# Spectral block and squared-ReLU layer: the middle part with pair 0's casts on ScalarE, pair 6's stage 4 from Z, pair 7's stage 4 by sums, and written orders

## The chip, the cores and the metric

One core of a Trainium2 chip. The metric is the device time of one execution in microseconds (us), the median of several runs. A profile covers one execution; its span runs from the first to the last instruction. Below, PE is TensorE, DVE is VectorE, ACT is ScalarE, POOL is GpSimd, and SP issues the DMAs.

## What is computed

The input is x, 2048 rows of 512 (bf16). The first half is a layer norm, a two-dimensional real Fourier transform over rows and columns, a product with a complex weight for each frequency, the transform back, and x added. The second half is a layer norm and a dense layer with a squared ReLU, and its input added.

```
def _A_ref(x, w_r, w_i):
    X = jnp.fft.rfft2(x.astype(jnp.float32), axes=(-2, -1))
    X = X * (w_r + 1j * w_i)
    return jnp.fft.irfft2(X, s=(S, D), axes=(-2, -1)).astype(jnp.bfloat16)
def _B_ref(x, w1, b1, w2, b2):
    h = jnp.einsum("bsd,df->bsf", x, w1) + b1
    r = jnp.where(h > 0, h, 0)
    return jnp.einsum("bsf,fd->bsd", r * r, w2) + b2
h  = x + _A_ref(_layernorm(x), A_w_r, A_w_i)
h2 = h + _B_ref(_layernorm(h), B_w1, B_b1, B_w2, B_b2)
```

F, the width of the dense layer, is 1792.

## The kernel before, in words

The transforms are products with tables of sines and cosines, which the kernel makes at its start. Rows are held as 128 partitions of 16 groups. The Fourier part has six stages:

- Stage 1 (line 409) multiplies x with a table that also holds the norm's scale, and leaves Bt. Up to about 21 us.
- Stage 2 (line 502, tile p2) and its cast to U (line 514, ScalarE; halves of pairs 0 and 1 on both engines).
- Stage 3 (line 553; pair 0: line 535, tile p3) and its cast to AB or X (lines 543 and 582).
- X by a sum and a difference of AB's halves (line 587, VectorE; pairs 5 to 7 get X from TensorE and skip it), the product m of X with the weights W (line 601, VectorE), Z, the two parts of the complex product (line 613, VectorE), and the folds M, sum and difference of Z's halves (line 621, VectorE; pair 0 has none).
- Stage 4 (line 634, tile p4): products of M with the tables EI; pair 0 reads Z. Its cast to T2 (line 659) is on ScalarE, for pair 7 on ScalarE and VectorE, a small part first (T2a), the rest later.
- Stages 5 and 6 (lines 709 to 807) end the transform and add x; the first two groups have a form of their own. Then the dense layer: line 904 the first product, line 917 the ReLU, line 922 the square, line 933 the second product, line 943 the sum, one DMA out for each group.

The loop of line 488 goes over eight pairs, pair 0 being rows 0 and 8 of the frequency axis and pair p the rows p and 16-p. Stages 2 and 3 of pair 0 and stage 2 of pair 1 are emitted earlier ("first").

The order on each engine is the work of a planner, the class Plan (line 34). Every operation is a task with an engine, an assumed duration, what it reads and writes, a priority and, where it takes a buffer, a pool with a number of buffers ("mm" and "sg" are PSUM, 3 and 2 in the middle; U, X, m, Z and M have 2 buffers each, AB 3). `run` (line 89) takes again and again the task that by its own reckoning can start first; "lag" is what it adds for a DMA's landing. The order in which tasks are taken is the order of the instructions on their engine, and the waits follow from the tiles. Where the planner sees TensorE idle, `warm` (line 235) and `bank` (line 687) put small products of zeros in front of a new PSUM tile, called fillers below, whose number follows from the planned gap. The middle part is everything between the `run` of line 491 and that of line 676. There the planner's order has M of pair 6 on VectorE ahead of pair 7's m, and pair 7's stage 4 (two tiles, one for each value of r) in this form:

```
for lt in (2 * half, 2 * half + 1):
    r, e = lt // 2, lt % 2
    ...
    for u in range(2):
        mm(o, lhsT=mv[:, u, r, e, :], rhs=EI[:, 1 - u:3 - u, pr, :], start=(u == 0), stop=(u == 1))
```

Each tile needs both folds (u is the fold).

Of the kernel before, what the change touches and what calls it, by code (L numbers as in the profile page):

```python
# [9 lines left out]
ALU = mybir.AluOpType  # L10
# [5 lines left out]
P = 128  # L16
# [17 lines left out]
class Plan:  # L34
# [13 lines left out]
    def add(self, eng, w, fn, reads=(), writes=(), prio=0.0, alloc=None, at=0.0, shared=False, lag=0.0,  # L48
            uses=(), order=()):
        many = isinstance(eng, tuple)  # L50
        ways = dict(zip(eng, w)) if many else {eng: w}
        t = dict(many=many, eng=None, ways=ways, w=0.0, fn=fn, reads=list(reads), writes=list(writes), prio=prio, alloc=alloc, at=at,
                 shared=shared, lag=lag, end=None, order=list(order), n=len(self.tasks))
        self.tasks.append(t)
        for k in t["writes"]:
            self.made.setdefault(k, []).append(t)
        for k in set(t["reads"]) | set(t["writes"]) | set(uses):
            self.use.setdefault(k, []).append(t)
# [30 lines left out]
    def run(self):  # L89
        left = {}  # L90
        for t in self.tasks:
            if t["end"] is None:
                for e in t["ways"]:
                    left.setdefault(e, []).append(t)
        for ts in left.values():
            ts.sort(key=lambda t: (t["prio"], t["n"]))
        while any(left.values()):
            best = None
            for e, ts in left.items():
                cand = []  # L100
                for t in ts:
                    r = self.ready(t, e)
                    if r is None:
                        continue
                    if t["alloc"]:
                        s, _ = self.slot(t["alloc"][0])
                        if s is None:
                            continue
                        r = max(r, s)
                    r = max(r, self.free[e])  # L110
                    cand.append((r, t))
                    if r <= self.free[e] + 1e-9:
                        break
                pick = None
                if cand:
                    first = min(r for r, _ in cand) + self.SLACK
                    pick = next(c for c in cand if c[0] <= first)
                if pick and (best is None or pick[0] < best[0] or (pick[0] == best[0] and e == "DVE")):
                    best = (*pick, e)
            if best is None:  # L120
                raise RuntimeError("no task can start: " + str([(list(t["ways"]), t["writes"]) for ts in left.values()
                                                                for t in ts][:6]))
            r, t, e = best
            t["eng"], t["w"] = e, t["ways"][e]
            if t["alloc"]:
                tag, key = t["alloc"]
                _, old = self.slot(tag)
                if old is not None:
                    self.held[tag].remove(old)
                self.held[tag].append(key)  # L130
            self.gap = r - self.free[e]
            t["end"] = r + t["w"]
            self.free[e] = t["end"]
            for k in t["ways"]:
                left[k].remove(t)
            self.log.append((r, t["end"], e, t["writes"]))
            t["fn"](*([e] if t["many"] else []))
# [3 lines left out]
def kernel(  # L141
# [21 lines left out]
    WSC = 2.0 / (S * D)  # L163
    L = D // 2
# [35 lines left out]
    EI = fwd.tile([P, 3, 9, P], BF16, name="EI")  # L200
    CN = fwd.tile([P, 7, P], BF16, name="CN")
# [74 lines left out]
    for i in range(2):  # L276
        add("SP", 1.0, lambda i=i: (sy.dma_start(W[:, i], wv[i][:, 0:8, 1:L + 1]),
                                        sy.dma_start(W[:, 2 + i, 0], wv[i][:, 8, 1:L + 1])), writes=[("Wn", i)],
            prio=8 + i, at=1.0, lag=6.0)
    for i in range(2):  # L280
        add("SP", 1.0, lambda i=i: sy.dma_start(W[:, 2 + i, 1:8], wx[i][:, ::-1]), reads=[("wx", i)], writes=[("Wr", i)],
            prio=10 + i, lag=6.0)
# [163 lines left out]
    def tr_dma(i, dst, src, dep, prio):  # L446
        add("SP", 2.5, lambda: sy.dma_start(dst, src, transpose=True), reads=dep, writes=[("EI", i)], prio=prio, lag=4.0)
# [9 lines left out]
    PE0, PE1, PES = 5, 8, 1  # L457
    BY_PE = tuple(range(PE0, PE1, PES))
    dve(0.25, lambda: ve.tensor_scalar(CN[:, 0:len(BY_PE)], EF[:, 1, PE0:PE1:PES], -1.0, None, ALU.mult), 75.0, reads=["EF1"],
# [11 lines left out]
    def mid_tasks():  # L471
        def b1t():
# [4 lines left out]
            order=["EF2", ("X", 0, 0)], writes=[("EI", 2)])  # L477
        act(1.07, lambda: sin_of(flat(GI[:]), lo(flat(fiI[:]))), 142.0, reads=["fiI"], order=[("p3", 4)], writes=["GI"])
# [9 lines left out]
    for pr, first in ((0, 1), (1, 1), *((p, 0) for p in range(8))):  # L488
# [45 lines left out]
        if pr == 0 and first:  # L534
# [8 lines left out]
            def ea0(u):  # L543
                X = buf(fwd, ("X", 0), "AB", [P, 2, 2, 256], BF16, 3) if u == 0 else T["X", 0]
                COPY[("ACT", "DVE")[u]](flat(X[:, u]), T["p3", 0, u][:])
            for u in range(2):
                add("PE", 0.46, lambda u=u, s3z=s3z: s3z(u), reads=[("U", 0, u), "EF0", "EF1", "EF2"], order=[("p3", 0, j) for j in range(u)],
                    writes=[("p3", 0, u)], prio=z + 1, alloc=("sg", ("p3", 0, u)))
                add(("ACT", "DVE")[u], (0.59, 0.66)[u], lambda u=u, ea0=ea0: ea0(u), prio=z + 1, reads=[("p3", 0, u)],
                    order=[("X", 0, 0)] * u, writes=[("X", 0), ("Xu", u)] + [("X", 0, 0)] * (1 - u),  # L550
                    alloc=None if u else ("AB", ("X", 0)))
        elif pr > 0 and not first:
# [32 lines left out]
            act(0.93, ea, z + 1, reads=[("p3", pr)], writes=[ab], alloc=("AB", ab))  # L585
            if ab[0] == "AB":
# [6 lines left out]
                for h in range(2):  # L593
                    dve(0.34, lambda pr=pr, h=h: bf(pr, h), z, reads=[("AB", pr)],
                        order=[("Xh", pr)] * h,
                        writes=[("X", pr)] + [("Xh", pr)] * (1 - h), alloc=("X", ("X", pr)) if h == 0 else None)
# [9 lines left out]
        for u in range(2) if pr == 0 else ():  # L606
            dve(0.61, lambda u=u, prod=prod: prod(0, u, 1), z, reads=[("Xu", u), ("Wn", 0), ("Wn", 1)], uses=[("X", 0)],
                order=["mh"] * u, writes=[("m", 0)] + ["mh"] * (1 - u), alloc=None if u else ("m", ("m", 0)))
# [7 lines left out]
        for r in range(2):  # L616
            dve(0.34, lambda pr=pr, r=r: zz(pr, r), z, reads=[("m", pr)],
                order=[("Zh", pr)] * r,
                writes=[("Z", pr)] + [("Zh", pr)] * (1 - r), alloc=("Z", ("Z", pr)) if r == 0 else None)
        if pr > 0:  # L620
# [8 lines left out]
            for h in range(2):  # L629
                dve(0.34, lambda pr=pr, h=h: fold(pr, h), z, reads=[("Z", pr)],  # L630
                        order=[("Mh", pr)] * h,
                    writes=[("M", pr)] + [("Mh", pr)] * (1 - h), alloc=("M", ("M", pr)) if h == 0 else None)

        def s4(pr=pr, half=0):
            if pr == 7:
                pt = sg_tile(("p4", pr, half))
            else:
                pt = mm_tile(("p4", pr)) if half == 0 else T["p4", pr]
            for lt in (2 * half, 2 * half + 1):
                r, e = lt // 2, lt % 2  # L640
                k = lt % 2 if pr == 7 else lt
                o = pt[:, 256 * k:256 * k + 256]
                if pr == 0:
                    zv = T["Z", 0][:].rearrange("p u r (j e) -> p u r e j", e=2)
                    for u, k1 in ((0, 0), (1, 8)):
                        ou = o[:, P * u:P * u + P]
                        mm(ou, lhsT=zv[:, u, r, e, :], rhs=EI[:, 1, k1, :], start=True, stop=False)
                        mm(ou, lhsT=zv[:, u, 1 - r, e, :], rhs=EI[:, 2 if r == 0 else 0, k1, :], start=False, stop=True)
                else:
                    mv = T["M", pr][:].rearrange("p u r (j e) -> p u r e j", e=2)  # L650
                    for u in range(2):
                        mm(o, lhsT=mv[:, u, r, e, :], rhs=EI[:, 1 - u:3 - u, pr, :], start=(u == 0), stop=(u == 1))  # L652
        for h in range(2):
            add("PE", 0.46, lambda pr=pr, h=h, s4=s4: s4(pr, h),
                reads=[("M" if pr else "Z", pr), ("EI", 0), ("EI", 1), ("EI", 2)], order=[("p4", pr, 0)] * h,
                writes=[("p4", pr), ("p4", pr, h)], prio=z + 32 * (pr < 5),
                alloc=("sg", ("p4", pr, h)) if pr == 7 else ("mm", ("p4", pr)) if h == 0 else None)

        def et(eng=sc.copy, pr=pr, a=0, b=G, l0=0, l1=4):
            dst = T2[:, l0:l1, a:b, 2 * pr:2 * pr + 2, :].rearrange("p l g q s -> p l q g s")  # L660
            src = T["p4", 7, l0 // 2] if pr == 7 else T["p4", pr]
            eng(dst, src[:].rearrange("p (l q g s) -> p l q g s", q=2, g=G, s=8)[:, :, :, a:b])
        if pr < 7:
            act(0.97, et, z + 3, reads=[("p4", pr)], writes=["T2", "T2a"])
        else:
            for h in range(2):
                eng = ("ACT", "DVE")[h]
                add(eng, (0.24, 0.22)[h], lambda et=et, h=h, eng=eng: et(COPY[eng], 7, 0, 2, 2 * h, 2 * h + 2), prio=z,
                    reads=[("p4", 7, h)], writes=["T2a"])
                add(eng, (0.52, 0.6)[h], lambda et=et, h=h, eng=eng: et(COPY[eng], 7, 2, G, 2 * h, 2 * h + 2), prio=z + 90,  # L670
                    reads=[("p4", 7, h)], order=["T2a"], writes=["T2"])
# [4 lines left out]
    plan.run()  # L676
# [52 lines left out]
    for c, (a, b) in enumerate(CHUNKS):  # L729
# [3 lines left out]
        for g in range(a, b):  # L733
            z = late + g
            if c > 0:
# [18 lines left out]
                for i in range(2):  # L754
                    dve(0.36, lambda g=g, i=i: lv1(g, i), z, reads=[("p5", g), ("od", g)],
                        order=[("qh", g)] * i + [("un", 1)] * (c == 1),
                        writes=[("q", g), ("qh", g)] if i == 0 else [("q", g)], alloc=("qb" if g in BY_PE2 else "q", ("q", g)) if i == 0 else None)
# [16 lines left out]
                else:  # L774
# [11 lines left out]
                    for k in range(4):  # L786
                        dve(0.25, lambda g=g, k=k: lv2(g, k), z, reads=[("q", g)], order=[("Rh", g)], writes=[("R", g)])
# [9 lines left out]
        if c == 0:  # L797
            for g in range(2):
# [9 lines left out]
                for k in range(3):  # L808
# [3 lines left out]
                        writes=[("py", g, k)], prio=-5000.0 + g - 50 * (k == 0), alloc=("sg", ("py", g)) if k == 0 else None)  # L812
# [21 lines left out]
                add(("ACT", "DVE")[g], (0.6, 0.7)[g], un0, reads=[("r2", 0, g), ("n2", 0, g)], writes=[("un", g)] + ["una0"] * (1 - g),  # L834
# [16 lines left out]
        else:  # L851
# [8 lines left out]
            for g in range(a, b):  # L860
                def un(e, g=g, a=a, c=c):
# [9 lines left out]
                    writes=[("un", g)] + [("una", a)] * (g == a), prio=z, shared=True, alloc=("u2", ("u", c)) if g == a else None)  # L871
            for g in range(a, b):
# [3 lines left out]
                def turn(c=c, i=g - a):  # L876
# [3 lines left out]
                    writes=[("UT", c)] + [("UTh", c)] * (g == a), prio=z, alloc=("UT", ("UT", c)) if g == a else None)  # L880
            for g in range(a, b):
# [9 lines left out]
                def et2(e, c=c, g=g, i=g - a):  # L891
# [3 lines left out]
                    writes=[("UT", c)] + [("UTh", c)] * (g == a), prio=z, alloc=("UT", ("UT", c)) if g == a else None)  # L895

        for f in range(NF):
# [24 lines left out]
            def sqr(c=c, f=f, n=n):  # L922
# [4 lines left out]
                writes=[("act", c, f), ("act", c)], alloc=("act", ("act", c)) if f == 0 else None)  # L927
# [53 lines left out]
```

## Time and profile before

| | |
|---|---|
| Time, median of 3 runs | 161.3 us (160.69, 161.30, 161.52) |
| Span of the profiled execution | 159.2 us; the page gives no other time for it |
| TensorE busy | 152.4 us, 1026 products recorded |
| VectorE busy | 120.6 us, 325 instructions |
| ScalarE busy | 102.2 us, 187 instructions |
| GpSimd busy | 32.9 us, 83 instructions |
| Granted TensorE clock | 1.000 over the span |
| Middle part | about 21.5 to 46.4 us of the span |

A row of the timeline gives the start in us, the time it takes, the engine, the line, the operation, out<-in with partitions x elements, how many instructions the row joins (x2), and in brackets the idle time of the engine ahead of it with what ended it. A row of the chain of waits gives start, length and what the time was spent on; "issue" is time in which the engine waited for nothing that the profile shows. A matmul's end is modelled.

### The profile page before, as it was taken

The numbers are of one execution on the slowest core, as the hardware profiler recorded it, in microseconds if no ns is written. First come the engines' busy times: TensorE is split into PE (matmuls) and PEld (weight loads), VectorE is DVE, ScalarE is ACT, GpSimd is POOL, SyncE is SP. The second block draws the span as 40 slices with busy tenths as digits, with TensorE's granted clock in tenths as the row PEclk, the third lists the DMA queues.
The fourth block names the chain that finished last, engine by engine and source line by source line (L and its number), as shares of the span: only waits on it lengthen the run. The fifth ranks groups of instructions, "written<-read, shape, count | busy, mean of one in ns | idle before, by whom it ended". The sixth has DMA issues, their size and how long they took to land.

```text
span 159.2 us, 2899 instructions
## 1 busy us (share of the span) xinstructions
PE 152.4 (96%) x1026; PEld 92.2 (58%) x1035; DVE 120.6 (76%) x325; ACT 102.2 (64%) x187; POOL 32.9 (21%) x83
## 2 busy tenths in 40 slices
PE   6999999999988999999999999999999999999992
PEld 4587876777666876565644544444544444565471
DVE  6999999999967996889863898992599962285221
ACT  8989689998976897297900889530488820188100
POOL 8798700000000024022230004440002240000000
PEclk9999999999999999999999999999999999999999
DMA  5958999992000001102332000224100212010011
GB/s 137 326 185 236 210 272 223 399 353 77 0 4 0 0 4 35 35 33 33 37 64 68 33 0 4 57 44 132 33 2 4 55 43 66 33 35 4 0 66 33
DMA packets 21018, 13.43 MB, mean 84 GB/s; under 512 B 9739, under 2 KB 19723, under 8 KB 21003
## 3 DMA queue, kind: packets, MB, share of 16 engines
q1 hardware_dynamic: 21002, 13.25, 30.7%
q8 instruction: 8, 0.13, 0.4%
q14 instruction: 8, 0.06, 0.1%
HBM read 8.92 MB, written 3.01 MB: 75 GB/s over the span
## 4 chain that ended last, share of the span: by engine, by line
PE 70%; DVE 18%; DMA 4%; issue 3%; SPq 1%; ACT 0%; POOL 0%; DVEq 0%
PE po L936 30%; PE sg L907 20%; PE ph L907 10%; DVE m L605 5%; DMA xs<-in_A_x_dram 4%; DVE Z L615 4%; DVE st L387 3%; DVE M L626 2%; DVE M L628 2%; DVE X L591 2%; PE pp L762 1%; PE pp L769 1%; SPq L266 1%; PE s_p L507 1%; PE s_p L652 1%
## 5 line engine op out<-in xcount | busy, mean ns | idle before, releaser
L936 PE MATMUL po<-W,act 128*128 128x512 bf16 (+1 forms) x229 | 48.7, 366 | 0.5
L919 ACT ACTIVATE rl<-sg,b1f 128x384 bf16<-128x384 f32 (+2 forms) x46 | 27.3, 602 | 21.8 <-PE sg L907 20.6
L907 PEld LDWEIGHTS <-W 128*128 128x128 bf16 x288 | 26.8, 98 | 19.6 <-issue 0.2
L907 PE MATMUL sg<-UT,W 128*128 128x384 bf16 (+2 forms) x184 | 37.2, 337 | 0.0
L936 PEld LDWEIGHTS <-act 128*128 128x128 bf16 x238 | 23.2, 98 | 24.1
L925 DVE TENSOR_TENSOR act<-rl 128x384 bf16<-128x384 bf16 (+2 forms) x70 | 25.0, 366 | 6.5 <-ACT rl L919 6.0
L945 DVE TENSOR_TENSOR ot<-po,hb 128x512 bf16<-128x512 f32 (+1 forms) x17 | 11.2, 659 | 21.0 <-PE po L936 20.7
L854 POOL TENSOR_SCALAR rs<-ss 128x1 f32<-128x1 f32 x14 | 5.5, 394 | 91.5 <-ACT junk L674 91.5
L919 ACT ACTIVATE rl<-ph,b1f 128x512 bf16<-128x512 f32 (+2 forms) x23 | 13.9, 602 | 10.0 <-PE ph L907 9.4
L907 PE MATMUL ph<-UT,W 128*128 128x512 bf16 (+3 forms) x96 | 19.9, 330 | 0.1
L790 DVE TENSOR_TENSOR hs<-pp,xs 128x512 bf16<-128x512 f32 x14 | 9.7, 690 | 2.3 <-PE pp L762 1.3
L674 ACT ACTIVATE junk<-hs,nm 128x512 bf16<-128x512 bf16 x14 | 10.0, 713 | 0.1
L486 PE MATMUL m_p<-U,EF 128*128 128x512 bf16 (+1 forms) x46 | 9.5, 337 | 0.0
L387 DVE BATCH_NORM_STATS2 st<-xs 128x6 f32<-128x512 bf16 x14 | 9.0, 673 | 0.6 <-DMA xs<-in_A_x_dram 0.6
L785 DVE TENSOR_TENSOR R<-q 128x127 bf16<-128x127 f32 x40 | 9.4, 283 | 0.0
L794 DVE TENSOR_TENSOR hb<-hs,b2b 128x512 f32<-128x512 bf16 x14 | 9.2, 683 | 0.0
L237 PEld LDWEIGHTS <-fz 128*128 128x128 bf16 x80 | 6.4, 110 | 4.6 <-issue 2.6
L856 POOL TENSOR_TENSOR rs<-rs,mhalf 128x1 f32<-128x1 f32 x14 | 8.3, 594 | 1.2
L584 ACT CAST AB<-m_p 128x1024 bf16<-128x1024 f32 x7 | 7.1, 1019 | 1.2 <-PE m_p L486 1.1
L752 DVE TENSOR_TENSOR q<-pp,od 128x256 f32<-128x256 f32 x20 | 7.6, 414 | 0.0
L507 PEld LDWEIGHTS <-Bt 128*128 128x128 bf16 x64 | 6.2, 98 | 1.5 <-DVE Bt L442 0.2
L652 PEld LDWEIGHTS <-M 128*128 128x128 bf16 x56 | 5.2, 98 | 3.1 <-DVE M L626 1.4
(160 smaller groups left out, 229.5 us busy)
## 6 DMA issues: line engine op xcount, KB each, us to landing
W<-in_B_w_dram SPq DMA_DIRECT2D x2, 1792.0 KB, 10.5
out_dram<-ot SPq DMA_DIRECT2D x15, 128.0 KB, 1.8
xs<-in_A_x_dram SPq DMA_DIRECT2D x4, 256.0 KB, 3.8
xs<-in_A_x_dram SPq DMA_DIRECT2D x2, 512.0 KB, 6.8
W<-wx SPq DMA_DIRECT2D x2, 448.0 KB
W<-in_A_w_r_dram SPq DMA_DIRECT2D x1, 512.0 KB, 8.2
W<-in_A_w_i_dram SPq DMA_DIRECT2D x1, 512.0 KB, 6.2
wx<-in_A_w_r_dram SPq DMA_DIRECT2D x1, 448.0 KB
```

The source lines that it names most:

```text
L387: ve.bn_stats(st[:], xs[:, g, :])
L486: mm(o.rearrange("p (j i e) -> p j i e", e=2, i=RUN), lhsT=w, rhs=U[:, q, s].rearrange("p (j e i) -> p j i e", e=2, i=RUN), **k)
L674: sc.activation(junk[:], src, ACT.Square, bias=nm1[:, g:g + 1], accum_out=ss2[:, g:g + 1])
L785: ve.tensor_tensor(o, x, y, (ALU.add, ALU.subtract, ALU.subtract, ALU.add)[k])
L790: dve(0.66, lambda g=g: ve.tensor_tensor(hs[:, g, :], T["p6", g][:], xs[:, g, :], ALU.add), z, reads=[("p6", g)], writes=[("hs", g)])
L794: add(("DVE", "POOL")[HBP], (0.62, 1.3)[HBP], lambda g=g: (ve, gp)[HBP].tensor_tensor(hb[:, g, :], hs[:, g, :], b2b[:], ALU.add), prio=lat ...
L856: pool(0.57, lambda p0=p0, p1=p1: gp.tensor_tensor(rs2[:, p0:p1], rs2[:, p0:p1], mhalf[:, 0:p1 - p0], ALU.pow), z, reads=[("sd", c, k)], w ...
L907: mm(p[:, P * i0:P * i1], lhsT=W1[:, d, bass.ts(f, P)], rhs=T["UT", c][:, i0:i1, d, :], start=(d == 0), stop=(d == ND - 1))
L919: sc.activation(r[:, 0:P * n], T["ph", c, f][:, 0:P * n], ACT.Relu, bias=b1f[:, f:f + 1], scale=1.0)
L925: ve.tensor_tensor(t[:, f, 0:P * n], r[:, 0:P * n], r[:, 0:P * n], ALU.mult)
L936: mm(p[:, cs], lhsT=T["act", c][:, f, bass.ts(i, P)], rhs=W2[:, f, cs], start=(f == 0), stop=(f == NF - 1))
L945: ve.tensor_tensor(o[:, cs], T["po", g, h][:, cs], hb[:, g, cs], ALU.add)
```

## The change

It touches the planner and the middle part; the stages before and behind keep their code, and only names are added there.

- Tasks get names, and `run` takes a written order for each engine; the middle part runs by such an order for PE, ACT and DVE.
- Pair 0: both halves of the cast after stage 3 are on ScalarE (before: one on ScalarE, one on VectorE).
- Pair 6 has no folds. Its stage 4 reads Z, with 16 products instead of 8, and needs a negated table EN (128x256), which ScalarE makes from EI. The first part needs only the first half of Z.
- Stage 4 of pairs 1 to 5 and 7 sums over the folds: a first part with M's first half into all outputs, a second part with M's second half. For pair 7 each part is in two pieces, one for each tile.
- The planner's assumed DMA lags change.

```
-                COPY[("ACT", "DVE")[u]](flat(X[:, u]), T["p3", 0, u][:])
+                sc.copy(flat(X[:, u]), T["p3", 0, u][:])
...
+        for pr in BY_Z:
+            act(0.37, lambda pr=pr: sc.activation(EN[:, BY_Z.index(pr)], EI[:, 0:2, pr], ACT.Identity, scale=-1.0), 84.0,
+                reads=[("EI", 0), ("EI", 1)], writes=[("EI", 3, pr)])
...
-        if pr > 0:
+        if pr > 0 and pr not in BY_Z:
             def fold(pr=pr, h=0):
...
-        def s4(pr=pr, half=0):
+        def s4(pr, part, lts):
+            key = ("p4", pr, "t", lts[0] // 2) if pr == 7 else ("p4", pr)
+            pt = T[key] if part else (sg_tile if pr == 7 else mm_tile)(key)
+            src = T["M" if pr and pr not in BY_Z else "Z", pr][:].rearrange("p u r (j e) -> p u r e j", e=2)
+            for lt in lts:
...
+                elif pr in BY_Z:
+                    for u in range(2):
+                        i = 1 if r == part else 0 if u != r else 2
+                        mm(o, lhsT=src[:, u, part, e, :], rhs=EI[:, i:i + 2, pr, :] if i < 2 else EN[:, BY_Z.index(pr)],
+                           start=part == 0 and e == 0 and u == 0, stop=part == 1 and e == 1 and u == 1)
                 else:
+                    mm(o, lhsT=src[:, part, r, e, :], rhs=EI[:, 1 - part:3 - part, pr, :],
+                       start=part == 0 and e == 0, stop=part == 1 and e == 1)
...
+    MID = {
+        "PE": "p2-2-0 p2-2-1 p3-1 p2-3-0 p2-3-1 p3-2 p2-5-0 p2-5-1 p3-3 p2-6-0 b1 p2-4-0 p2-4-1 p3-5 "
+             "p2-6-1 p3-4 p4-0-0 p4-0-1 p4-1-0 p4-1-1 p2-7-0 p2-7-1 p4-2-0 p4-2-1 p3-6 p3-7 p4-3-0 "
+             "p4-3-1 p4-5-0 p4-5-1 p4-4-0 p4-4-1 p4-6-0 p4-6-1 p4-7-0a p4-7-0b p4-7-1a p4-7-1b",
+        "ACT": "U-2 AB-1 U-3 AB-2 U-5 AB-3 EI-2 b1f U-4 AB-5 U-6 AB-4 T2-0 T2-1 U-7 GI EI-3-6 AB-6 T2-2 "
+              "AB-7 T2-3 T2-5 sqrt T2-4 T2-6 T2a-0 T2b-0",
+        "DVE": "m-0-0 m-0-1 Z-0-0 Z-0-1 X-1-0 X-1-1 m-1 X-2-0 Z-1-0 Z-1-1 X-2-1 M-1-0 M-1-1 X-3-0 m-2 "
+              "X-3-1 Z-2-0 Z-2-1 m-3 M-2-0 Z-3-0 Z-3-1 M-2-1 M-3-0 X-4-0 m-5 X-4-1 Z-5-0 Z-5-1 m-4 "
+              "M-5-0 M-5-1 M-3-1 Z-4-0 Z-4-1 m-6 M-4-0 Z-6-0 M-4-1 m-7 Z-6-1 Z-7-0 Z-7-1 M-7-0 M-7-1 "
+              "T2a-1 T2b-1",
+    }
+    plan.run(MID)
```

In a name like M-4-1 the first number is the pair and the second the half; EI-3-6 is the negated table of pair 6.

## The prediction

> **What bounds the kernel now.** I read the share of the span by engine and line first, then the chain of waits between 17 and 50 us, then each engine's instructions in order of time over the stretch that the change touches.
>
> ```profile
> PE 70%; DVE 18%; DMA 4%; issue 3%; SPq 1%; ACT 0%; POOL 0%; DVEq 0%
> PE po L936 30%; PE sg L907 20%; PE ph L907 10%; DVE m L605 5%; DMA xs<-in_A_x_dram 4%; DVE Z L615 4%; DVE st L387 3%; DVE M L626 2%; DVE M L628 2%; DVE X L591 2%; PE pp L762 1%; PE pp L769 1%; SPq L266 1%; PE s_p L507 1%; PE s_p L652 1%
> ```
>
> TensorE carries the last two thirds (the dense layer, lines 907 and 936). The middle, which the change rewrites, hangs on VectorE alone: lines 605, 615, 591, 626 and 628. The chain of waits shows it without a break:
>
> ```profile
> 21.53 0.06 DVE AB L545
> ...
> 24.92 1.24 DVE m L605
> 26.16 0.02 issue
> 26.18 0.77 DVE Z L615 x2
> ...
> 45.02 0.35 DVE M L628
> 45.37 0.04 issue
> 45.42 0.94 PE s_p L652 x7
> 46.36 0.28 PE pp L690 x5
> 46.64 0.76 PE pp L712 x6
> ```
>
> So from 21.53 to 45.36 us the end is set by VectorE, then by pair 7's stage 4, five filler products and stage 5. What the middle gains, the dense layer starts earlier: its weights landed at 32.1 and 38.3 us, so no transfer holds it, and I let the gain pass whole.
>
> The single rows that I use, VectorE and then ScalarE:
>
> ```profile
> 21.53 0.69 DVE L545 CAST AB<-s_p 128x512 bf16<-128x512 f32 x1 [0.18 <-PE s_p L486]
> 22.14 1.28 DVE L605 TENSOR_TENSOR m<-AB,W 128x1024 bf16<-128x1024 bf16 x2
> 23.46 0.76 DVE L615 TENSOR_TENSOR Z<-m 128x512 bf16<-128x512 bf16 x2
> 24.14 0.75 DVE L591 TENSOR_TENSOR X<-AB 128x512 bf16<-128x512 bf16 x2
> 24.92 1.23 DVE L605 TENSOR_TENSOR m<-X,W 128x2048 bf16<-128x2048 bf16 x1
> ```
>
> ```profile
> 21.10 0.59 ACT L545 CAST AB<-s_p 128x512 bf16<-128x512 f32 x1 [0.28 <-PE s_p L486]
> 21.58 1.17 ACT L476 ACTIVATE EI<-EI 128x1152 bf16<-128x1152 bf16 x1
> 22.83 1.01 ACT L584 CAST AB<-m_p 128x1024 bf16<-128x1024 f32 x1
> ```
>
> From such rows: a VectorE operation on 512 elements takes 0.415 us, but the next starts 0.335 after it (the two Z: 0.76 in all); a product m takes 1.215, pitch 1.135; half an m, pitch 0.60; a ScalarE cast of 1024 takes 1.015, pitch 0.91. An operation that needs the result of the one just ahead starts 0.035 after its end, not 0.08 before it (Z ends at 24.22, X began at 24.14; but m ends at 26.15 and its Z starts at 26.18). Such a pair loses 0.115; with a separate wait instruction between, as for the folds at 41.81 and 44.60, 0.18. TensorE starts 128x256 products every 0.109 us and 128x512 ones every 0.216.
>
> **The change, step by step.** Up to 21.3 us the instruction order is unchanged, and on SP's and GpSimd's queues throughout, DMAs included; the new lags only steer the planner.
>
> 1. *Pair 0's second cast leaves VectorE.* It frees 0.61 there. But the first half of m waits for the first cast, which ScalarE still ends at 21.69. For that hand-over I take 0.055, the nearest row being ScalarE to TensorE (a cast ends 24.76, its product starts 24.82): m at 21.74 instead of 22.14, minus 0.40. ScalarE does the second cast at 21.58 to 22.17, in time for 22.34. m, m, Z, Z (0.60, 0.72, 0.335, 0.335) leave VectorE free at 23.74.
>
> 2. *A new stall ahead of X of pair 1.* The written order makes TensorE do both halves of pair 2's stage 2 before pair 1's stage 3: eight products from 21.33, the last ending at 22.37, and ScalarE must cast U of pair 2 first (22.47 with its wait instructions). Only then, 0.91 later, comes pair 1's cast AB, 23.39 to 24.40, against 22.83 to 23.85 before. On VectorE everything is queued behind X: it waits from 23.74 to 24.46, and m of pair 1 starts at 25.25 instead of 24.92: plus 0.33. The 0.40 is gone and more. (The second half of W for this m landed at 24.57, so it doesn't hold it.)
>
> 3. *Pair 6's two folds go:* 2 x 0.335, minus 0.67.
>
> 4. *The written order parts dependent neighbours.* After pair 1's m, the page of before pays 0.115 at two Z behind their m (26.18, 35.99), at M (26.98), at m (34.73) and at Z (43.74), and 0.18 at the M of 41.81 and 44.60: 0.93. In the new order another operation stands between nearly all; only pair 7's M directly follows its Z (0.115). Minus 0.81. Here the Trainium skill speaks against the change: "VectorE: DVE Perf Modes", section "The DRAIN you can't avoid", says that the next operation doesn't start until the pipe is empty and that a semaphore costs nothing extra. By that rule this term is nil, and the sum ends near 161.4. The rows above decide otherwise (X starts 0.08 before Z's end), so I take 0.81.
>
> 5. *Pair 6 reads Z, at a price: a new wait.* In the built program, the second half of pair 6's Z waits for the last product of the first part of its stage 4, which reads the first half; the halves interleave in one tile. VectorE runs without stall from 25.25 through 27 small operations and 7 m: 27 x 0.335 + 7 x 1.135 = 17.0, to 42.27. The wait ends later: pair 4's M ends at 41.21; TensorE, in its written order, does four products of pair 4 (to 41.70) and then pair 6's eight, the last starting at 42.47 and ending at 42.74; Z starts at 42.78. Plus 0.51. Pair 7's Z and M, the end of the stage, are queued behind it.
>
>    The other costs of this edit: eight more products on TensorE (0.87), of which the path sees what the wait holds; the negated table on ScalarE, 128x256, between 0.37 (the EO cast of that size) and 0.47; I take 0.47, hidden by the 1.1 us that AB of pair 6 is early for its m, and up to 0.1 more without that cover.
>
> Together at the last M: 0.33 - 0.67 - 0.81 + 0.51 = -0.64, so about 44.7 instead of 45.36. Adding the new order forward, 42.78 + 3 x 0.335 + 0.115 + 0.335 + 0.418, gives 44.65.
>
> 6. *Pair 7's stage 4 by sums.* Four of its eight products need only the first M. They start at 44.4, so after the second M four are left instead of eight: 0.4 less. But ten filler products (five before) now stand between it and stage 5. The last product ends at 45.45, VectorE's small cast at 45.7, stage 5 could go on at 45.76; the fillers occupy TensorE to 45.84, and its second product, the one that needs VectorE, starts at 45.95. Before, 46.68. Of the 0.4 the fillers and the cast's latency leave about 0.1. T2 of pair 6 on ScalarE (44.33 to 45.34) ends just as pair 7's first tile is ready, so it costs nothing, but has no slack. The swapped EO casts (0.37 against 0.42) are within 0.05 either way; I take nothing. The 21 fillers that go from the middle stood in TensorE's idle time: nothing.
>
> Sum: -0.64 - 0.1 = **-0.7 us**, of a profiled span of 159.2, hence 158.5. The page gives no other time for that execution; the three runs, 160.69 to 161.52, lie 1.5 to 2.3 above this span, which I take as unchanged. On the median 161.3 this makes **160.6 us**, 0.43% less.
>
> **Rivals.**
> - *The hold in step 5 is short or absent* (the sum's only stall behind a product that is done within a few tenths). Then Z follows at 42.3, the stage ends 0.5 earlier, and T2 of pair 6 moves along: -1.2, 160.1. For it: at 41.3 to 42.3 VectorE has a whole m to cover TensorE. Against: the wait is in the program, and the twelve products take 1.3 us by their rows.
> - *ScalarE eats the gain.* It has 0.59 + 0.47 more, and by my sums no idle time from 22.47 to 43.6: 19 casts at 0.91, tables and the table load. X of pairs 2 and 3 have 0.1 and 0.3 us of slack, T2 of pair 6 0.7. Two rows of before show casts of 1.06 and 1.07 (30.45 and 31.36). If all took that, 19 x 0.05 = 0.95 collects, and 0.3 to 0.6 of it lands on the path: 161.1.
> - *ScalarE becomes the bound, slower:* the same engine, with the place at the late casts (T2 of pairs 4 and 6). It decides from a mean pitch above 0.99: 19 x 0.08 = 1.5, less 0.7 of slack, cancels the gain. At 1.05, 19 x 0.14 = 2.7, less 0.7, against -0.7: 162.6. Against it: no cast of before is above 1.07 (pitch 0.96).
>
> **How the numbers follow.** A measurement can tell about 0.5% (0.8 us) from no change, so the limits are 160.5 and 162.1. Main sum: 0.55, spread 160.2 to 161.0, a little under half below 160.5. Short hold: 0.20, all below. ScalarE eats the gain: 0.14, no change. Slower: 0.11. Faster 0.25 + 0.20 = 0.45; same 0.30 + 0.14 = 0.44; slower 0.11. The range 159.8 to 161.5 takes in the first three and the bounds of the hand-over and the table, and leaves most of the last out.
>
> **What would show it.** VectorE idle for 0.7 us before X at 24.5, and 0.5 before a Z near 42.8, ended by TensorE; the last M ending at 44.7; no loss between Z and M elsewhere; the second product of stage 5 near 45.95; ScalarE without idle time from 22.5. I am wrong if pair 1's AB ends before 24.0 (faster), if the dependent pairs cost 0.115 wherever they stand (no gain), or if VectorE waits for ScalarE after 30 us (slower).

## The result, and the profile after

| | before | changed |
|---|---|---|
| Time, median of 4 runs | 161.09 us (160.69 to 161.52) | 160.26 us (159.92 to 160.37) |
| Ratio, 95% interval | | 0.9938 (0.9917 to 0.9960) |
| Span of the profiled execution | 159.2 us | 158.4 us (this execution took 160.21) |
| VectorE / ScalarE busy | 120.6 / 102.2 us | 119.0 / 102.5 us |

The change gains 0.83 us, 0.4 to 0.8% by the interval; 0.7 us was forecast. The shares by engine and line in the changed kernel:

```profile
PE 74%; DVE 15%; DMA 4%; issue 3%; SPq 1%; ACT 1%; POOL 0%; ACTq 0%
PE po L965 31%; PE sg L936 20%; PE ph L936 10%; DMA xs<-in_A_x_dram 4%; DVE Z L624 3%; DVE m L614 3%; DVE st L393 3%; DVE X L600 2%; PE m_p L516 2%; PE pp L788 1%; DVE M L635 1%; PE pp L795 1%; SPq L272 1%; DVE M L637 1%; PE s_p L516 1%
```

VectorE's share of the chain fell from 18% to 15%. TensorE's stage 2 (line 516, "PE m_p") now has 2%; before, one stretch of 0.87 us of it stood in the chain, too little for this list. The chain of waits between 17 and 50 us shows where (start, length, what):

```profile
22.42 0.86 PE m_p L495 x4
23.28 0.89 PE m_p L516 x8
24.17 0.03 ACTq L526
24.20 0.24 ACT AB L593
24.44 0.02 issue
24.46 0.77 DVE X L600 x2
...
41.27 0.61 PE m_p L662 x4
41.88 0.89 PE m_p L659 x8
42.77 0.02 issue
42.79 1.10 DVE Z L624 x3
...
44.40 1.05 PE s_p L662 x8
45.45 0.56 PE pp L716 x10
46.00 0.65 PE pp L738 x6
```

Before, VectorE alone stood in the chain from 21.53 to 45.36. Now the chain leaves it twice, at the two places that steps 2 and 5 named: ahead of X of pair 1 (TensorE and ScalarE, to 24.46) and ahead of the second half of pair 6's Z (TensorE, to 42.79). VectorE's own rows, with the idle time in brackets:

```profile
21.77 1.29 DVE L614 TENSOR_TENSOR m<-AB,W 128x1024 bf16<-128x1024 bf16 x2 [0.36 <-ACT AB L554]
23.09 0.76 DVE L624 TENSOR_TENSOR Z<-m 128x512 bf16<-128x512 bf16 x2
24.46 0.76 DVE L600 TENSOR_TENSOR X<-AB 128x512 bf16<-128x512 bf16 x2 [0.61 <-ACT AB L593]
25.25 1.22 DVE L614 TENSOR_TENSOR m<-X,W 128x2048 bf16<-128x2048 bf16 x1
...
41.13 1.21 DVE L614 TENSOR_TENSOR m<-AB,W 128x2048 bf16<-128x2048 bf16 x1
42.79 1.09 DVE L624 TENSOR_TENSOR Z<-m 128x512 bf16<-128x512 bf16 x3 [0.45 <-PE m_p L659]
43.92 0.42 DVE L635 TENSOR_TENSOR M<-Z 128x512 bf16<-128x512 bf16 x1
44.26 0.42 DVE L637 TENSOR_TENSOR M<-Z 128x512 bf16<-128x512 bf16 x1
```

Between 25.25 and 42.34 no row has a bracket, so VectorE never stands idle there. And ScalarE, where the rivals had placed trouble:

```profile
25.22 1.04 ACT L593 CAST AB<-m_p 128x1024 bf16<-128x1024 f32 x1
26.12 1.06 ACT L526 CAST U<-m_p 128x1024 bf16<-128x1024 f32 x1
27.02 1.07 ACT L593 CAST AB<-m_p 128x1024 bf16<-128x1024 f32 x1
27.93 1.22 ACT L482 ACTIVATE EI<-EI 128x1152 bf16<-128x1152 bf16 x1
```

The casts take 1.04, 1.06, 1.07, yet start 0.90 to 0.91 apart. A row's length is not what the engine pays for it.

### The profile page after: what moved, and what is told of

It is laid out like the page before. It is cut to its first block, busy times and chain, and to the rows that moved or that the text cites. A ratio compares the mean times of both kernels' runs of the same rounds, so it can differ in the third digit from the quotient of the medians.

```text
span 158.4 us, 2890 instructions
## 1 busy us (share of the span) xinstructions
PE 152.0 (96%) x1027; PEld 91.9 (58%) x1027; DVE 119.0 (75%) x322; ACT 102.5 (65%) x189; POOL 33.1 (21%) x83
## 4 chain that ended last, share of the span: by engine, by line
PE 74%; DVE 15%; DMA 4%; issue 3%; SPq 1%; ACT 1%; POOL 0%; ACTq 0%
PE po L965 31%; PE sg L936 20%; PE ph L936 10%; DMA xs<-in_A_x_dram 4%; DVE Z L624 3%; DVE m L614 3%; DVE st L393 3%; DVE X L600 2%; PE m_p L516 2%; PE pp L788 1%; DVE M L635 1%; PE pp L795 1%; SPq L272 1%; DVE M L637 1%; PE s_p L516 1%
## 5 line engine op out<-in xcount | busy, mean ns | idle before, releaser
L965 PE MATMUL po<-W,act 128*128 128x512 bf16 (+1 forms) x238 | 50.0, 366 | 0.0
L880 POOL TENSOR_SCALAR rs<-ss 128x1 f32<-128x1 f32 x14 | 6.1, 435 | 90.5 <-ACT junk L689 90.5
L243 PEld LDWEIGHTS <-fz 128*128 128x128 bf16 x59 | 5.0, 113 | 4.2 <-issue 2.3
L516 PE MATMUL m_p<-GF,Bt 128*128 128x256 bf16 x56 | 7.4, 273 | 0.0
L677 ACT CAST T<-m_p 128x1024 bf16<-128x1024 f32 x7 | 7.1, 1057 | 0.5 <-PE m_p L659 0.5
```

The lines of the kernel that those rows point to most:

```text
L516: mm(puv[:, e, :], lhsT=Bt[:, 2 * t + 1 - e, 2 * pr + q, :], rhs=gfv[:, t, :, e, :], start=(t == 0), stop=(t == 1))
L965: mm(p[:, cs], lhsT=T["act", c][:, f, bass.ts(i, P)], rhs=W2[:, f, cs], start=(f == 0), stop=(f == NF - 1))
```

## The experiments

There are twelve kernels, in three groups of four (e1 to e4, e5 to e8, e9 to e12), each group on one chip together with the kernel before, whose median was 161.12, 161.15 and 161.30 there. A ratio compares within a group; a difference of medians between kernels of different groups, or to the changed kernel, is one between chips. VectorE's last cast U (line 517 before, 526 after) starts anywhere between 20.46 and 21.46 us in the fourteen profiles, so I compare three stretches behind it inside each profile:

- A: from the start of that cast to the start of m of pair 1;
- B: from there to the end of the last M;
- C: from there to the second product of stage 5, the one that waits for VectorE's cast T2.

What follows, up to the end of the span, takes 112.48 to 112.50 us in all fourteen profiles. So the gain of the middle passes whole through the dense layer, as the prediction took it, and the stretches can be added.

| kernel | A | B | C | median us | ratio to before (95%) |
|---|---|---|---|---|---|
| before | 4.26 | 20.44 | 1.32 | 161.09 | |
| changed | 4.54 | 19.42 | 1.28 | 160.26 | 0.9938 (0.9917 to 0.9960) |
| e1 planner's order | 4.30 | 19.90 | 1.59 | 160.87 | 0.9980 (0.9961 to 0.9998) |
| e2 cast back | 4.67 | 19.43 | 1.27 | 160.45 | 0.9953 (0.9934 to 0.9972) |
| e3 halves apart | 4.54 | 18.97 | 1.28 | 159.79 | 0.9913 (0.9886 to 0.9941) |
| e4 folds back | 4.54 | 19.64 | 1.09 | 160.37 | 0.9951 (0.9931 to 0.9972) |
| e5 neighbours | 4.74 | 20.05 | 1.10 | 160.65 | 0.9977 (0.9963 to 0.9991) |
| e6 AB of pair 1 first | 4.01 | 20.73 | 1.27 | 160.92 | 0.9988 (0.9977 to 0.9998) |
| e7 pair 7 whole | 4.54 | 19.43 | 1.22 | 160.19 | 0.9940 (0.9927 to 0.9953) |
| e8 five fillers | 5.35 | 19.43 | 1.09 | 160.02 | 0.9939 (0.9917 to 0.9961) |
| e9 apart, five fillers | 4.67 | 18.96 | 1.09 | 159.59 | 0.9891 (0.9863 to 0.9918) |
| e10 order only | 4.83 | 19.63 | 1.21 | 160.40 | 0.9947 (0.9927 to 0.9968) |
| e11 W early | 4.54 | 19.42 | 1.28 | 160.37 | 0.9944 (0.9922 to 0.9965) |
| e12 all three | 4.54 | 18.96 | 1.09 | 159.70 | 0.9902 (0.9876 to 0.9929) |

Only the intervals of e1, e5 and e6 lie apart from that of the changed kernel. For the others the stretches of the one profile of each carry the verdict. Where A is above 4.54 (e2, e5, e8, e9, e10), m of pair 1 waited for W in that execution; see the last section.

**Theory and rival.** The theory is the prediction's ledger: the written order pays, by parting dependent neighbours on VectorE, and pair 6's saved folds are mostly eaten by the hold, the wait of step 5. The rival: what pays is the 1.28 us of work taken from VectorE (pair 0's cast 0.61, pair 6's folds 0.67).

**e10, the written order alone**: pair 0's cast is back on VectorE, pair 6 has folds, and pair 7's tiles come one after the other. The summed form of stage 4 and the planner's new lags stay.

```
-    BY_Z = (6,)
+    BY_Z = ()
-                sc.copy(flat(X[:, u]), T["p3", 0, u][:])
+                COPY[("ACT", "DVE")[u]](flat(X[:, u]), T["p3", 0, u][:])
-  m-6 M-4-0 Z-6-0 M-4-1 m-7 Z-6-1 Z-7-0 ...   p4-7-0a p4-7-0b p4-7-1a p4-7-1b
+  m-6 M-4-0 M-4-1 Z-6-0 Z-6-1 m-7 M-6-0 M-6-1 Z-7-0 ...   p4-7-0a p4-7-1a p4-7-0b p4-7-1b
```

> The written order alone: the changed kernel with pair 0's second cast back on VectorE, pair 6's folds restored (stage 4 from M, no negated table) and pair 7's stage 4 one tile after the other. Theory A (each of the three edits is worth next to nothing in this order, the order carries the gain): 0 to 0.2 above the changed kernel, 160.3 to 160.5; the last M about 24.15 us after the start of the last cast U on VectorE (23.96 in the changed kernel, 24.70 before). Rival B (the 1.28 us of work taken from VectorE carry it): 160.9 to 161.2, within 0.2 of before.

160.40: by medians this kernel has 0.69 of the 0.83 us, by the ratios 0.53 of 0.62%. Stretch B is 19.63 against 20.44 before, with the same VectorE operations in it and no bracket in either. One of the seven places that step 4 lists, first before, then in e10:

```profile
40.95 0.75 DVE L615 TENSOR_TENSOR Z<-m 128x512 bf16<-128x512 bf16 x2
41.81 0.43 DVE L626 TENSOR_TENSOR M<-Z 128x512 bf16<-128x512 bf16 x1
```

```profile
40.83 0.75 DVE L624 TENSOR_TENSOR Z<-m 128x512 bf16<-128x512 bf16 x2
41.50 1.22 DVE L614 TENSOR_TENSOR m<-AB,W 128x2048 bf16<-128x2048 bf16 x1
42.63 0.42 DVE L635 TENSOR_TENSOR M<-Z 128x512 bf16<-128x512 bf16 x1
```

Before, M stands behind the two Z that it needs and starts 0.86 after the first of them; two pitches are 0.67, so 0.19 is lost. In e10 m of pair 7 stands between: it starts 0.67 after the first Z, and M 1.13 after m, which is the pitch of m, so nothing is lost. The 0.81 agrees with step 4. That it does so to the hundredth is luck: the gaps of before add up to 0.98 by their rows, not 0.93, and in e10 the pair that stays (Z and M of pair 7) costs 0.19, not 0.115. Against the 0.81, A is 0.28 longer without its wait for W (the stall of step 2, which the order makes). C is 0.11 shorter, which may come from the summed form of stage 4. The last M came 24.46 after the cast U, 0.3 more than expected, as m of pair 1 had waited 0.3 for W. The rival falls: B got shorter with none of its work gone.

**e5, neighbours.** Z of pairs 1, 2, 5 directly behind their m, and m of pairs 3, 4 behind their X.

```
-  m-1 X-2-0 Z-1-0 Z-1-1 X-2-1 ... m-2 X-3-1 Z-2-0 Z-2-1 m-3 ... m-5 X-4-1 Z-5-0 Z-5-1 m-4
+  m-1 Z-1-0 Z-1-1 X-2-0 X-2-1 ... m-2 Z-2-0 Z-2-1 X-3-1 m-3 ... m-5 Z-5-0 Z-5-1 X-4-1 m-4
```

> The changed kernel, with four moves in VectorE's written order that set dependent operations side by side: Z of pairs 1, 2 and 5 directly behind their m, and m of pairs 3 and 4 directly behind the second half of their X; the same operations otherwise. Theory A: five dependent neighbours at 0.115 each, 0.55 to 0.6 in all; last M near 45.25, time 0.4 to 0.6 above the changed kernel (160.65 to 160.85). Rival B (an operation waits for the pipe of the one ahead anyway, and a semaphore costs nothing extra): no change, within 0.1.

B grew by 0.63, 0.125 for each of the five. The median grew by 0.39, as C is 0.2 shorter: the planner sets seven fillers here instead of ten. Its rows:

```profile
28.84 1.22 DVE L614 TENSOR_TENSOR m<-X,W 128x2048 bf16<-128x2048 bf16 x1
30.10 0.76 DVE L624 TENSOR_TENSOR Z<-m 128x512 bf16<-128x512 bf16 x2
30.77 0.42 DVE L600 TENSOR_TENSOR X<-AB 128x512 bf16<-128x512 bf16 x1
31.23 1.22 DVE L614 TENSOR_TENSOR m<-X,W 128x2048 bf16<-128x2048 bf16 x1
```

Z needs m and starts 1.26 after it; X needs nothing of Z's and starts 0.67 after two Z (0.335 each); m needs X and starts 0.46 after it. No bracket shows, as a gap of 0.04 isn't listed and the rest is overlap that is lost. Step 4 weighed a section of the Trainium skill ("VectorE: DVE Perf Modes", "The DRAIN you can't avoid"), and took only its first half: it also says that a next operation that is not held starts earlier. These rows agree with that half, as independent operations overlap by 0.08. That a semaphore costs nothing extra doesn't carry over to an operation that waits for the one just ahead: that costs 0.125 here.

**e1, the planner's own order**, all edits kept: `plan.run()` for `plan.run(MID)`.

> All edits of the change, but the middle part in the planner's own order instead of the written one. Theory A (the written order earns its keep by parting dependent neighbours): six or more pairs of dependent VectorE operations come back at 0.115 to 0.18 each; part of it is offset by an earlier cast AB of pair 1 (0.3 less stall). Last M at 44.95 to 45.05 instead of 44.67, time 160.5 to 160.7 (ratio to before 0.996 to 0.998). Rival B (order is worth nothing on VectorE, as each operation waits for the pipe of the one ahead to empty; the gain is all in removed work): the same as the changed kernel, 160.2 to 160.3, last M within 0.1 of 44.67.

160.87: 0.6 us slower than the changed kernel, and above the 160.5 to 160.7 expected. B is 0.48 longer (the gaps return, less the hold), A 0.24 shorter, as expected; but C is 0.31 longer, which I had not foreseen. ScalarE tells why:

```profile
41.01 1.01 ACT L593 CAST AB<-m_p 128x1024 bf16<-128x1024 f32 x1 [1.16 <-PE m_p L495]
42.05 1.28 ACT L488 ACT_TABLE_LOAD   x1
43.34 0.21 ACT L488 ACTIVATE junk<-eps 128x1 bf16<-128x1 f32 x1
43.45 2.82 ACT L677 CAST T<-m_p 128x1024 bf16<-128x1024 f32 x3
46.15 0.67 ACT L677 CAST T<-s_p 128x64 bf16<-128x64 f32 x2
```

Pair 7's AB comes late, after 1.16 us of waiting for TensorE. The table load stands behind it, and three casts T2 are then queued ahead of pair 7's, which starts at 46.15 although its products are there from about 45.5. The written order of TensorE and ScalarE is thus worth 0.3 here. The other way round, e1 shows what the edits bring without that order: its interval, 0.9961 to 0.9998, lies just below no change.

**e3, halves apart.** Pair 6's Z with r ahead of u in the tile, so that the halves don't interleave.

```
-            ve.tensor_tensor(Z[:, :, r], T["m", pr]...
+            ve.tensor_tensor(Z[:, r] if pr in BY_Z else Z[:, :, r], T["m", pr]...
```

(and the same in stage 4's reading).

> The changed kernel, with pair 6's Z laid out half by half (r ahead of u in the tile), so that the second half's write doesn't overlap the span of addresses that the first part of stage 4 reads. Theory A (the hold on the second half of Z costs about 0.45): Z follows m of pair 7 without a wait near 42.27, the last M ends near 44.2 instead of 44.67, time 159.8 (0.45 less than the changed kernel). Rival B (the hold is hidden, since stage 4 of pair 6 and its cast T2 on ScalarE are next in line): the last M comes earlier but stage 5 doesn't, less than 0.15 gained.

159.79: 0.47 faster than the changed kernel, with B 0.45 shorter and C unchanged. The Z follows m without a bracket:

```profile
41.13 1.23 DVE L614 TENSOR_TENSOR m<-AB,W 128x2048 bf16<-128x2048 bf16 x1
42.26 1.10 DVE L624 TENSOR_TENSOR Z<-m 128x512 bf16<-128x512 bf16 x3
43.47 0.43 DVE L635 TENSOR_TENSOR M<-Z 128x512 bf16<-128x512 bf16 x1
```

Z starts 0.53 earlier; 0.08 of it goes to M of pair 7, which now loses 0.2 behind its Z instead of 0.12. The hold of step 5 was a matter of layout only: no element that the first part reads is written by the second half.

**e4, folds back** (pair 6 with folds, no negated table).

```
-    BY_Z = (6,)
+    BY_Z = ()
-  m-6 M-4-0 Z-6-0 M-4-1 m-7 Z-6-1 Z-7-0
+  m-6 M-4-0 M-4-1 Z-6-0 Z-6-1 m-7 M-6-0 M-6-1 Z-7-0
```

> The changed kernel with pair 6's two folds restored, its stage 4 from M in 8 products, no negated table; M of pair 6 follows m of pair 7 in the written order. Theory A: the folds cost 0.67 on VectorE, but the hold of 0.45 is gone and M of pair 7 pays 0.06 more, so the last M ends near 44.9; five fillers fewer ahead of stage 5 give most of that back: time within 0.15 of the changed kernel, so reading Z is worth next to nothing in this form. Rival B (the two folds are worth their 0.67): time 0.5 to 0.7 above the changed kernel, 160.8 to 160.95.

160.37, 0.11 above the changed kernel. B is 0.22 longer (0.67 for the folds, less the 0.45 of the hold), C 0.19 shorter, with five fillers instead of ten. As built, reading Z earns next to nothing. In e3's layout it earns its 0.67 in B (18.97 against 19.64).

**e2, cast back** (pair 0's second cast on VectorE; the second diff line of e10).

> The changed kernel, with pair 0's second cast after stage 3 back on VectorE. Theory A: the stall ahead of pair 1's X, which waits for ScalarE's AB at 24.43, swallows the 0.61 us; both m of pair 0 start 0.4 later, X of pair 1 still at 24.46, VectorE's wait there falls from 0.61 to 0.2, and the time is that of the changed kernel (within 0.1 of 160.26). Rival B: VectorE's busy time is what counts, and 0.4 to 0.6 us are lost (160.7 to 160.9).

B and C are unchanged. VectorE's wait ahead of X of pair 1 shrinks from 0.61 to 0.19, as expected:

```profile
24.58 0.76 DVE L600 TENSOR_TENSOR X<-AB 128x512 bf16<-128x512 bf16 x2 [0.19 <-ACT AB L593]
25.51 1.23 DVE L614 TENSOR_TENSOR m<-X,W 128x2048 bf16<-128x2048 bf16 x1 [0.16 <-DMA W<-wx]
```

In this profile the cast's 0.61 us replace waits: 0.42 of that stall, and 0.18 ahead of the first m (a bracket of 0.36 in the changed kernel, of 0.18 ahead of the cast here). The median, 160.45, is 0.19 above the changed kernel, more than the 0.1 expected, with overlapping intervals. A is 0.13 longer because W landed at 25.38, which is no cost of the cast. Whether the cast itself costs 0 or 0.2 in the median stays open.

**e6, AB of pair 1 first.**

```
-        "PE": "p2-2-0 p2-2-1 p3-1 ...      "ACT": "U-2 AB-1 U-3 ...
+        "PE": "p2-2-0 p3-1 p2-2-1 ...      "ACT": "AB-1 U-2 U-3 ...
```

> The changed kernel, with pair 1's stage 3 ahead of the second half of pair 2's stage 2 on TensorE, and pair 1's cast AB ahead of pair 2's U on ScalarE, as before the change. Theory A: the stall ahead of X of pair 1 shrinks from 0.61 to below 0.2, but then m of pair 1 waits for the second part of W, which landed at 25.07 in the profile of the changed kernel, so it starts at 25.1 to 25.2 (0.1 gained at most), and AB of pair 2 comes 0.6 later, so a new stall of 0.6 to 0.7 arises at X of pair 2; time 0.4 to 0.6 above the changed kernel. Rival B (the stall at X of pair 1 is a plain loss): 0.4 to 0.6 below the changed kernel, 159.7 to 159.9.

160.92, 0.66 slower than the changed kernel. The stall moves from pair 1 to pair 2 and grows:

```profile
24.23 0.76 DVE L600 TENSOR_TENSOR X<-AB 128x512 bf16<-128x512 bf16 x2
25.03 1.23 DVE L614 TENSOR_TENSOR m<-X,W 128x2048 bf16<-128x2048 bf16 x1
27.27 0.43 DVE L600 TENSOR_TENSOR X<-AB 128x512 bf16<-128x512 bf16 x1 [1.02 <-ACT AB L593]
```

A is 0.53 shorter, where 0.1 at most was expected: W had landed at 24.27 in this execution and so didn't limit it. B is 1.31 longer. So the stall of step 2 is the price of having pair 2 on time, not a plain loss.

**e7, pair 7 whole** (each tile waits for both folds; seven fillers).

```
+  "h" * (1 - h) * (pr < 7)          (pair 7's first part waits for all of M)
-  p4-7-0a p4-7-0b p4-7-1a p4-7-1b
+  p4-7-0a p4-7-1a p4-7-0b p4-7-1b
```

> The changed kernel, with pair 7's stage 4 one tile after the other, each waiting for both folds as before the change; the planner then sets seven fillers ahead of stage 5 instead of ten. Theory A: the split earns nothing in the changed kernel, since fillers and the cast take back its 0.4: within 0.1 of the changed kernel. Rival B: the split is worth its four products, 0.3 to 0.45 above the changed kernel.

160.19 against 160.26, and C is 0.05 shorter, with seven fillers instead of ten: the split earns nothing in the changed kernel.

**e8, five fillers.**

```
-        for _ in range(min(20, ...
+        for _ in range(min(5 if key == ("pd", 0, 1) else 20, ...
```

> The changed kernel with at most five fillers (ten in it) in the first tile of stage 5. Theory A: the fillers hold TensorE to 45.84 while VectorE's small cast is done at 45.71; with five, stage 5's second product starts 0.15 to 0.2 earlier and the time falls by as much, to about 160.1. Rival B (fillers stand in idle time and cost nothing, or keep the clock up): no change, or a lower granted clock and a later end.

160.02: C falls by 0.19, the median by 0.24, and the granted clock in the profile stays at 1.000. The profiled execution is one of 161.09, the slowest of six, in which W landed at 26.18 and m of pair 1 waited 0.84 for it (A 5.35). In its rows stage 5 follows the five fillers at once:

```profile
46.33 0.44 PE L716 MATMUL pp<-fz 128*128 128x128 bf16 x5
46.61 0.92 PE L738 MATMUL pp<-GI,T 128*128 128x256 bf16 x6
```

**e9 and e12, what gained, together; e11, W early.** e11 sends the second part of W ahead of the transposes of EI, by one more order constraint on the latter; e12 has this too.

```
+            order=[("Wr", 0), ("Wr", 1)])
```

> The changed kernel with pair 6's Z laid out half by half and five fillers ahead of stage 5: the two edits that gained, together. Theory A (they act at two places of one chain, so they add): 0.45 + 0.2, 159.6 to 159.7. Rival B (ScalarE, whose casts T2 of pairs 4 and 6 come right ahead, becomes the bound as the stage ends earlier): no more than halves apart alone gave (159.79).

> The changed kernel with the second part of W issued on SP ahead of the two transposes of EI, instead of between and behind them. The profiles so far show that part landing between 24.3 and 26.2 us, and m of pair 1 (25.25 in the changed kernel) waiting for it by 0.16, 0.24 and 0.84 in three of them. Theory A (the changed kernel has no slack there, so the landing costs in some executions): it lands 3 us earlier, m never waits for it, and the median falls by 0.1 to 0.2 (160.1), the spread of the runs too; EI is needed only near 28. Rival B: the landing is rarely late, no change; or the transposes land late and stage 4 waits, slower.

> The changed kernel with all three: pair 6's Z half by half, five fillers ahead of stage 5, the second part of W issued early. Theory A: 0.45 + 0.2 + 0.1 below the changed kernel, 159.5. Rival B: the early W moves nothing, 159.65.

e9 is the fastest kernel here: 159.59, 0.67 below the changed kernel, about the sum of e3 and e8 (B 0.46, C 0.19 shorter). In e11, W landed at 24.18 (changed: 25.09), not 3 us earlier, and m of pair 1 didn't wait for it; but the median is 160.37, no gain, and the runs spread no less (160.17 to 160.67). e12 lands W at 23.31 and takes 159.70, against 159.59 for e9 without it, and not the 159.5 that my theory expected. So landing W early gains nothing in the median. Why is open. It isn't that late landings are rare: of the nine profiles that have pair 2's stage 2 ahead of pair 1's stage 3 and W issued at its old place, five show m waiting for W, which made A longer by 0.13 to 0.81.

## Why the prediction was right

The steps, against the changed kernel's profile:

| step | forecast | measured |
|---|---|---|
| 1: first m | 21.74 | 21.77 |
| 2: X, and m of pair 1 | 24.46, 25.25 | 24.46, 25.25 |
| 3 and 5: folds less hold | -0.67 + 0.51 = -0.16 | -0.22 (e4) |
| 4: gaps parted | -0.81 | -0.81 (e10), 0.125 each (e5) |
| 5: Z of pair 6 | 42.78 | 42.79 |
| last M ends | about 44.7 | 44.67 |
| 6: second product of stage 5 | 45.95 | 45.95 |
| span | 158.5 | 158.4 |

- *Steps 1 and 2 were right, and so was their sign:* the moved cast earns nothing that the profile shows where the next wait is for ScalarE (e2).
- *Step 4 was the term that decided.* Without its 0.81 the sum would have been no gain. Its size held (e10), and so did its cause (e5). Read with its second half, the Trainium skill's section does not speak against the change, as the step says it does (e5).
- *Step 5's hold was right in cause, and near in size:* 0.51 forecast, 0.45 measured in B (e3). I forecast it without seeing that another layout avoids it.
- *Step 6:* the fillers and the cast's latency take back what the split gives (e7, e8); 0.04 of 0.4 is left where I said 0.1.
- *Agreement to the hundredth is in part luck.* The changed kernel's execution started the cast U 0.05 later than the one before (20.72 against 20.66), so in stretches A grew by 0.28, not 0.33, B fell by 1.02, not 0.97, and C fell by 0.04, not 0.1. The sum, -0.78 against -0.74, is right because each term is nearly right.
- *The size of the time:* 160.6 was forecast on a median of 161.3, and 160.26 against 161.09 measured. Of the 0.34 between them, 0.21 is the other median of before, which now has a fourth run. The other 0.13 is a gain of 0.83 where the sum had 0.7, which the interval covers.
- *The rivals:* the hold was not short (0.45 idle). ScalarE neither ate the gain nor became the bound. My working of these two was faulty in one term: it multiplied the longer casts (19 x 0.05) as if their length were paid, and took a cast of 1.07 to mean a pitch of 0.96. The profile before already said otherwise: its cast of 1.06 starts at 30.45 and the next one at 31.36, a pitch of 0.91. In the changed kernel casts up to 1.12 appear, and those that stand back to back start 0.89 to 0.91 apart. The two rivals had a chance of 0.25 together, which that row should have lowered.

Where the gain comes from is thus not where the change has most of its code: the edits that took 1.28 us from VectorE, with pair 7's split, are worth 0.14 in this order (e10: 0.21 in B, less 0.07 in C, and the same by medians), and the written order with the summed form of stage 4 is worth 0.69 by medians. The intervals of the two kernels overlap, so the 0.14 rests on one profile of each.

## What to carry to other kernels

On an engine that never stands still, look at starts, not at lengths: two neighbours that depend on each other cost an overlap and a hand-over that no idle-time column shows (0.125 us a pair in e5), and an operation that has to be done anyway, moved between them, takes that cost away. Before taking work off an engine, ask what it waits for next: a saving ahead of a wait can be lost in it, as the cast's 0.61 us went into two longer waits (e2). And where a tile's halves are made and read at different times, try laying them out one behind the other: here a wait for elements that nobody shared was gone with it (e3).

## What the runs showed of the hardware

- VectorE: independent neighbours of 128x512 overlap by 0.08 us (pitch 0.335 at a length of 0.415, changed kernel). A dependent pair loses 0.125 in e5, and 0.19 where M follows its two Z (41.81 before).
- ScalarE: casts of 128x1024 from PSUM took between 0.99 and 1.12 us in the changed kernel's profile, at a pitch of 0.89 to 0.91 where they stood back to back.
- DMA: in the twelve profiles that issue it at the same place of the program, the second part of W landed between 24.27 and 26.18 us. Most of that spread is the time of issue: the later of its two DMAs was issued between 19.15 and 20.76, and took 4.9 to 5.7 us from there to landing. In the five profiles in which m of pair 1 waited for it, m started 0.12 after the landing, after an idle time of up to 0.84 us. In the changed kernel's profile it landed 0.16 before m started, which leaves 0.04 of slack.
- TensorE: in the changed kernel it stood idle for 0.41 us ahead of pair 4's stage 4 and for 0.52 us ahead of the second part of pair 6's, at a granted clock of 1.000. With five fillers fewer (e8) the clock in the profile was 1.000 too.
